# A convolution followed by an MLP: the transfers and the Pool casts of the opening in another order

## The chip, the core and the metric

The kernel runs on one core of a Trainium2 chip. The metric is the device time of one execution in microseconds (us); a kernel is given by the median of its runs.

## What is computed

The reference has two stages. The first is a causal convolution over 7 tokens whose weights depend only on the head (8 heads of 24 channels): a softmax over the 7 taps of each head, then a weighted sum of the last 7 tokens. The second is a two-layer MLP with the activation h cos h.

```python
w = softmax(weight)                                   # 8 heads x 7 taps
out[b, s, h, g] = sum_k w[h, k] * x_pad[b, s + k, h, g]   # x: 8 x 4096 x 192, 6 zero rows in front
x = out.reshape(32768, 192)
h = x @ w_in                                          # 192 -> 2048
return (h * cos(h)) @ w_out                           # 2048 -> 192, fp32
```

x holds 25 MB, w_in and w_out 1.57 MB each, all fp32; the matmuls run in bf16.

## The kernel before

**Units and tiles.** The 32768 tokens are cut into 32 units of 1024 tokens (x is loaded and convolved by units) and 64 tiles of 512 tokens (the MLP runs by tiles, two to a unit). The convolution of a unit is a set of matmuls against banded matrices (tile `band`, 128 x 8 x 256, built once from the softmaxed taps). Its result (`ct`) is transposed to channel-major form (`cT`), which feeds the first MLP matmul (`mm1`, eight pairs of h per tile, steps h0 to h7). ACT computes a cosine by its Sin function (`cs`, s0 to s7), DVE multiplies (`g`), and the second matmul (`mm2_step`, written m8, m12 and so on) accumulates into two PSUM banks, which ACT empties and SP stores.

**Order.** Every engine's order is the order in which the program records its instructions. Strings set it for a tile: `PE_ORDER` and `ACT_ORDER` from the third tile on, `PE_FIRST` and `ACT_FIRST` for the first two. In them h is an `mm1` step, c and d are halves of the next unit's convolution (ec, ed empty them on ACT), r is the second half of unit 0, m is `mm2`, s is a cosine. Three PSUM tiles (`h_pool`) hold h in turn, so an `mm1` step waits for the DVE product three steps back.

**Who casts.** Inputs arrive as fp32 and are cast to bf16 by other engines: x by Pool (`cast_unit`, L188; a piece of unit 0 by ACT), w_in in four pieces of two column groups each (pieces 0:2 on DVE at L286, 2:4 on Pool at L331, 4:6 and 6:8 on Pool at L442), w_out in two pieces on Pool (L447). Pool also doubles `ct` for the transposition (`double_unit`, L256) and mends `cT` (L268).

**Transfers.** SP and ACT issue transfers, each into a queue of its own, and both queues share 16 DMA engines. An instruction on SP that waits holds all that SP issues after it. In the opening SP issues, in this order: the first half of x's unit 0 (0.39 MB), piece 0:2 of w_in (0.39 MB, two transfers of 64 partitions each), the second half of unit 0, piece 2:4, piece 4:8 (0.79 MB), and w_out (1.57 MB in four). ACT issues the taps and then all of x's unit 1 (0.79 MB) with its edge rows (0.1 MB). Each transfer signals on one of eight completion semaphores in turn, so it also waits until the transfer eight before it has landed.

**The first 40 us.** Three plus eleven dummy matmuls (`keep_warm`) run while the taps are softmaxed. `mask`, a 0/1 pattern built by Pool on 32 partitions and copied by DVE to the other three quarters (L143), is multiplied with the taps (`prod`, L276) and reduced (`diag`, L279); 16 small casts (L284) put `diag` into `band`, dealt in turn to DVE, ACT and Pool. `conv_first` convolves the first half of unit 0, and `turn_first` transposes it by matmuls. The second half is convolved in tile 0 (`conv_rest`, step r) and transposed by a DMA (`turn_unit`, L262). Behind that transposition SP loads units 2 and 3. All casts that follow stand on Pool in one line, in this order: second half of unit 0; w_in 2:4; the doubling of unit 0; w_in 4:6 and 6:8; unit 1; w_out twice; the doubling of unit 1; units 2 and 3.

Of the kernel before, what the change touches and what calls it, by code (L numbers as in the profile page):

```python
# [9 lines left out]
BF16 = mybir.dt.bfloat16  # L10
AF = mybir.ActivationFunctionType
ALU = mybir.AluOpType
# [4 lines left out]
def kernel(  # L17
# [8 lines left out]
    nc = tc.nc  # L26
    B, S, D = x.shape
    H, K = weight.shape
# [5 lines left out]
    NB = T // 128  # L34
# [12 lines left out]
    consts = ctx.enter_context(tc.tile_pool(name="consts", bufs=1))  # L47
# [13 lines left out]
    HQ = H // 4  # L61
# [18 lines left out]
    w_src = moe_w_in.rearrange("(m k) (t f) -> t m k f", k=NC, t=2)  # L80
    HP = NP // 2

    def load_w(j0, j1):
        for t in range(2):
            nc.sync.dma_start(out=w_f[64 * t : 64 * t + 64, :, j0:j1, :].rearrange("p k j f -> p k (j f)"),
                              in_=w_src[t, :, :, j0 * 128 : j1 * 128])

    load_unit(0, 0, NB)
    load_w(0, 2)
    load_unit(0, NB, UB)  # L90
    load_w(2, 4)
    load_w(4, 8)
    wo_f = consts.tile([128, NP, 2, D], FP32)
    wo_src = moe_w_out.rearrange("(i j p) d -> p j i d", i=2, p=128)

    def load_wo(q):
        for i in range(2):
            nc.sync.dma_start(out=wo_f[:, q * HP : (q + 1) * HP, i], in_=wo_src[:, q * HP : (q + 1) * HP, i])

    load_wo(0)  # L100
    load_wo(1)


    one = consts.tile([128, 1], FP32)
# [5 lines left out]
    def keep_warm(n):  # L110
        for _ in range(n):
# [26 lines left out]
    nc.gpsimd.affine_select(out=mask[0:32], in_=mask[0:32], compare_op=ALU.not_equal, fill=1.0, base=1 - K,  # L138
                            pattern=[[1, K], [1, E]], channel_multiplier=-1)
# [44 lines left out]
    def cast_unit(u, n0=0, n1=UB + 1, copy=nc.gpsimd.tensor_copy):  # L184
        bf[u] = xb0 if u == 0 else xbf_pool.tile([128, UB + 1, D], BF16, name="x_bf")

        o = 1 if u == 0 else 0
        copy(out=bf[u][:, n0 + o : n1 + o, :].rearrange("p n (h k r) -> p (n h) k r", k=NC, r=R),  # L188
             in_=x_tiles[u][:, n0:n1, :].rearrange("p n (h r k) -> p (n h) k r", k=NC, r=R))
# [76 lines left out]
    def mend_edges(u):  # L266
# [9 lines left out]
    nc.vector.tensor_tensor(out=prod, in0=mask.rearrange("p k (o e) -> p o e k", o=1).to_broadcast([128, HQ, E, K]),  # L276
                            in1=wn.rearrange("p h (o k) -> p h o k", o=1).to_broadcast([128, HQ, E, K]), op=ALU.mult)
    diag = consts.tile([128, HQ, E], FP32)
    nc.vector.tensor_reduce(out=diag, in_=prod, axis=mybir.AxisListType.X, op=ALU.add)  # L279

    three = [nc.vector.tensor_copy, nc.scalar.copy, nc.gpsimd.tensor_copy]
    for i in range(16):
        q, rows = divmod(i, 4)
        three[i % 3](out=band[32 * rows : 32 * rows + 32, HQ * q : HQ * (q + 1), 32 * rows : 32 * rows + E],  # L284
                     in_=diag[32 * q : 32 * q + 32])
    nc.vector.tensor_copy(out=w[:, :, 0:2], in_=w_f[:, :, 0:2])  # L286
    cast_unit(0, NB, UB)
# [41 lines left out]
    turn_first(0)  # L329
    turn_first(1)  # L330
    nc.gpsimd.tensor_copy(out=w[:, :, 2:4], in_=w_f[:, :, 2:4])  # L331

# [57 lines left out]
    def store(t, b0=0, b1=2):  # L390
# [13 lines left out]
    ACT_FIRST = ["s0a s0b s1 s2 s3 s4 s5 ed1 ed2 s6 ec1 ec2 s7", "s0 s1 s2 s3 s4 ed1 ed2 s5 s6 ec1 ec2 P s7"]  # L404

    HALVES = {"": (0, NB), "a": (0, NB // 2), "b": (NB // 2, NB)}
    step = 0
    for t in range(NT + 2):
        u, second = divmod(t, TPU)
        cu, cc = (u + TPU, second) if t >= TPU else (1 + t, 1)  # L410
        conv = {"c": conv_part(cu, cc, ring_banks if t else o_banks, t < TPU) if cu < NU else iter(())}
        if t < TPU:
            conv["d"] = conv_part(cu, 0, ring_banks if t else o_banks, True)
        act, done, h = (ACT_ORDER if t > 1 else ACT_FIRST[t]).split(), set(), {}

        def flush():
            while act:
                k = act[0]
                need = {"P": "p", "Q": "q", "e": k[1:2] + "2"}.get(k[0], "h" + k[1:])
                if need not in done:  # L420
                    return
                act.pop(0)
                if k == "P" and 0 <= t - 1 < NT:
                    evac(t - 1, 0)
                elif k == "Q" and 0 <= t - 2 < NT:
                    evac(t - 2, 1)
                elif k[0] == "e":
                    next(conv[k[1]], None)
                elif k[0] == "s" and t < NT:
                    gcu(t, int(k[1]), h.pop(k[1:]), *HALVES[k[2:]])  # L430

        for k in (PE_ORDER if t > 1 else PE_FIRST[t]).split():
            if k[0] == "h" and t < NT:
                h[k[1:]] = mm1(t, int(k[1]), *HALVES[k[2:]])
            elif k[0] in conv:
                next(conv[k[0]], None)
            elif k == "r":
                conv_rest()
                double_unit(0, NB, UB)
                turn_unit(0, NB, UB)  # L440
                for j in (4, 6):
                    nc.gpsimd.tensor_copy(out=w[:, :, j : j + 2], in_=w_f[:, :, j : j + 2])  # L442
                cast_unit(1)
                load_unit(2)
                load_edges(2)
                for q in range(2):
                    nc.gpsimd.tensor_copy(out=wo[:, q * HP : (q + 1) * HP], in_=wo_f[:, q * HP : (q + 1) * HP])  # L447
            elif k[0] == "m":
                for q in range(step, step + int(k[1:])):
                    mm2_step(q)  # L450
                step += int(k[1:])
            elif k[0] == "p":
                assert step % (2 * STEPS) == 0
            elif k[0] == "q":
                assert step % (2 * STEPS) == STEPS
            done.add(k)
            flush()

            if k == "q":
                if second == 0 and t and u + 1 < NU:  # L460
                    turn_unit(u + 1)
                    mend_edges(u + 1)
                if t == 1:
                    turn_unit(1)
                    cast_unit(3)
                    mend_edges(1)
                if second == 0 and u + 3 < NU:
                    cast_unit(u + 3)
                if second == 1 and t > 1 and cu < NU:
                    double_unit(cu)  # L470
                if t == NT + 1:
                    store(NT - 1, 1, 2)
            if k == "p":
                if t < NT + 1 and 0 <= t - 2:
                    store(t - 2)
                if t == NT:
                    store(NT - 1, 0, 1)
                if second == 1 and u + 4 < NU:
                    load_unit(u + 4)
                    load_edges(u + 4)  # L480
        if t == 0:
            double_unit(1)
            load_unit(3)
            load_edges(3)
            cast_unit(2)
        if t == 1:
            double_unit(2)
# [30 lines left out]
```

## Time and profile before

| | |
|---|---|
| median of 8 runs | 725.96 us (725.02 to 726.35) |
| the profiled execution: own time, span | 725.02 us, 723.3 us |
| time outside the span | 1.7 us |
| PE busy | 709.3 us (98% of the span) |
| DVE, ACT, Pool busy | 613.7 us, 617.2 us, 150.2 us |
| PE busy from 40 to 715 us | 674.44 of 675 us |
| moved | 86.04 MB, 119 GB/s in the mean |

All positions in the text are microseconds from the start of the span. The span and what lies around it make the execution's own time; the profiled execution is one of the faster ones of its kernel (0.94 us under the median), so a change is worked out inside the span and then set against the median. "Idle before" in a row is the time for which the engine stood still ahead of that instruction, and the arrow names what ended it; where several things were waited for, it names the one that came last.

### The profile page before, as it was taken

What the parts mean: (1) busy time and instruction counts of PE and PEld (TensorE: products, weight loads), DVE (VectorE), ACT (ScalarE), POOL (GpSimd) and SP (SyncE); (2) the same over time, 40 slices, a digit from 0 to 9 for tenths busy, and PEclk for the clock granted to TensorE, in tenths of its full rate; (3) what the DMA queues carried; (4) which work ended last, traced back from release to release, by engine and by line L of the source; (5) the groups of instructions that cost most, each with busy time, mean ns of one, the idle gap of its engine ahead of it and who ended that gap; (6) DMA issues with size and microseconds to landing.
All of it is one profiled execution on the core that took longest, in us unless ns stands there. A gap on an engine that the chain in (4) does not pass through costs nothing.

```text
span 723.3 us, 26324 instructions
## 1 busy us (share of the span) xinstructions
PE 709.3 (98%) x11826; PEld 530.7 (73%) x11826; DVE 613.7 (85%) x538; ACT 617.2 (85%) x781; POOL 150.2 (21%) x125
## 2 busy tenths in 40 slices
PE   7799999999999999999999999999999999999997
PEld 3477777777777777777777777777777777777776
DVE  6778888888888888888888888888888888888983
ACT  5788888888888888888888888888888888888883
POOL 3731122210222211122210222220222211121000
PEclk9999999999999999999999999999999999999999
DMA  9945444555443555443555443565443555424312
GB/s 211 225 122 138 105 117 91 127 144 138 105 117 89 129 143 139 100 119 93 128 144 140 104 116 91 127 144 139 105 117 90 128 143 139 101 71 91 76 46 68
DMA packets 184497, 86.04 MB, mean 119 GB/s; under 512 B 111680, under 2 KB 184000, under 8 KB 184384
## 3 DMA queue, kind: packets, MB, share of 16 engines
q1 hardware_dynamic: 183200, 83.47, 47.5%
q8 instruction: 92, 1.51, 0.8%
q10 hardware_dynamic: 1184, 0.89, 0.5%
q14 instruction: 21, 0.17, 0.1%
HBM read 31.36 MB, written 25.17 MB: 78 GB/s over the span
## 4 chain that ended last, share of the span: by engine, by line
PE 95%; DMA 2%; POOL 1%; DVE 1%; ACT 0%; SPq 0%; issue 0%; DVEq 0%; POOLq 0%
PE o_ps L376 46%; PE h L346 45%; PE h L199 3%; DMA w_f<-in_moe_w_in_dram 1%; DMA x_f<-in_x_dram 1%; POOL x_bf L188 1%; PE h L376 0%; DVE g L357 0%; ACT cs L353 0%; POOL w L442 0%; DVEq L513 0%; SPq L262 0%; SPq L75 0%; ACT o_sb L388 0%; DVE ct L304 0%
## 5 line engine op out<-in xcount | busy, mean ns | idle before, releaser
L357 DVE TENSOR_TENSOR g<-h,cs 128x1024 bf16<-128x1024 f32 (+1 forms) x513 | 603.8, 1218 | 95.7 <-ACT cs L353 91.0
L353 ACT ACTIVATE cs<-h 128x1024 bf16<-128x1024 f32 (+1 forms) x513 | 511.6, 1026 | 61.4 <-PE h L346 54.2
L376 PE MATMUL o_ps<-wo,g 64*128 64x192 bf16 x8128 | 423.9, 243 | 1.5 <-ACT o_sb L388 0.6
L376 PEld LDWEIGHTS <-g 64*128 64x128 bf16 x8192 | 362.2, 94 | 85.6 <-SPq L173 1.2
L346 PE MATMUL h<-cT,w 64*128 64x512 bf16 (+1 forms) x3078 | 399.7, 377 | 2.2 <-POOL w L442 1.9
L346 PEld LDWEIGHTS <-w 64*128 64x128 bf16 x3078 | 154.8, 94 | 88.0 <-POOL w L442 2.4
L268 POOL COPY cT<-cT 128x144 bf16<-128x144 bf16 x31 | 9.5, 307 | 497.7 <-DMA cT<-ct 377.1
L188 POOL CAST x_bf<-x_f 128x1728 bf16<-128x1728 f32 (+2 forms) x33 | 81.3, 2463 | 4.4 <-DMA x_f<-in_x_dram 4.4
L214 ACT CAST ct<-h 128x432 bf16<-128x432 f32 x120 | 56.4, 522 | 27.0 <-PE h L199 26.9
L388 ACT COPY o_sb<-o_ps 128x384 f32<-128x384 f32 x127 | 60.1, 473 | 4.9 <-PE o_ps L376 4.9
L256 POOL COPY ct<-ct 128x1728 bf16<-128x1728 bf16 (+1 forms) x32 | 51.3, 1602 | 24.1 <-ACT ct L214 20.1
L199 PE MATMUL h<-x_bf,band 64*128 64x216 bf16 (+1 forms) x472 | 42.7, 254 | 0.5 <-POOL x_bf L188 0.5
L199 PEld LDWEIGHTS <-band 64*128 64x128 bf16 (+1 forms) x496 | 22.6, 96 | 6.4 <-issue 3.8
L112 PE MATMUL o_ps<-zero 128*128 128x512 bf16 x14 | 5.3, 547 | 1.3 <-DVE zero L107 1.3
L376 PE MATMUL h<-wo,g 64*128 64x192 bf16 x64 | 5.8, 243 | 0.0
L112 PEld LDWEIGHTS <-zero 128*128 128x128 bf16 x14 | 1.6, 127 | 3.7 <-issue 2.1
L199 PE MATMUL o_ps<-x_bf,band 128*128 128x96 bf16 (+1 forms) x24 | 2.5, 271 | 1.8 <-POOL x_bf L188 1.8
L214 ACT CAST ct<-o_ps 128x432 bf16<-128x432 f32 (+1 forms) x6 | 2.4, 457 | 1.1 <-PE o_ps L199 1.1
L447 POOL CAST wo<-wo_f 128x1536 bf16<-128x1536 f32 x2 | 2.9, 1472 | 0.0
L122 ACT ACT_TABLE_LOAD x1 | 1.3, 1283 | 1.4 <-PEq L502 1.4
L312 PE MATMUL h<-ident,ct 128*128 128x128 bf16 x9 | 0.8, 221 | 1.7 <-DVE ct L304 1.2
L388 ACT COPY o_sb<-h 128x384 f32<-128x384 f32 x1 | 0.5, 478 | 2.4 <-PE h L376 2.4
(47 smaller groups left out, 28.5 us busy)
## 6 DMA issues: line engine op xcount, KB each, us to landing
out_dram<-o_sb SPq DMA_DIRECT2D x63, 384.0 KB
x_f<-in_x_dram SPq DMA_DIRECT2D x30, 768.0 KB
x_f<-in_x_dram SPq DMA_DIRECT2D x30, 96.0 KB
wo_f<-in_moe_w_out_dram SPq DMA_DIRECT2D x4, 384.0 KB
x_f<-in_x_dram SPq DMA_DIRECT2D x2, 384.0 KB
w_f<-in_moe_w_in_dram SPq DMA_DIRECT2D x4, 192.0 KB
x_f<-in_x_dram ACTq DMA_DIRECT2D x1, 768.0 KB
w_f<-in_moe_w_in_dram SPq DMA_DIRECT2D x2, 384.0 KB
```

Of the source, the lines that this page charges most:

```text
L112: nc.tensor.matmul(out=idle, lhsT=zero[:, 0:128], rhs=zero, start=True, stop=True)
L188: copy(out=bf[u][:, n0 + o : n1 + o, :].rearrange("p n (h k r) -> p (n h) k r", k=NC, r=R), in_=x_tiles[u][:, n0:n1, :].rearrange("p n (h ...
L199: return nc.tensor.matmul(out=ps[i // 2][:, 0 : (n1 - n0) * 2 * G].rearrange("p (n k i r) -> p i n k r", n=n1 - n0, k=NC, i=2)[:, i % 2], ...
L214: copy(o[:, :, 0, :], i[:, :, 0, :])
L256: nc.gpsimd.tensor_copy(out=ct[:, n0:n1, :, 1, :], in_=ct[:, n0:n1, :, 0, :])
L268: nc.gpsimd.tensor_copy(out=cT[u][:, 0:UB, :, 0 : K - 1], in_=cT[u][:, UB].rearrange("p c (n t) -> p n c t", t=16)[:, :, :, 8 : 8 + K - 1])
L346: nc.tensor.matmul(out=h[:, i, n0 * 128 : n1 * 128], lhsT=w[rows, k, j, :], rhs=c[rows, m0 + n0 : m0 + n1, k, :], start=(k == 0), stop=(k ...
L353: nc.scalar.activation(out=cs[:, :, part], in_=h[:, :, part], func=AF.Sin, bias=math.pi / 2.0, scale=1.0)
L357: nc.vector.tensor_tensor(out=g_tiles[t][:, 2 * j : 2 * j + 2, part], in0=h[:, :, part], in1=cs[:, :, part], op=ALU.mult)
L376: m = nc.tensor.matmul(out=o_ps[tt, b][:, si * D : (si + 1) * D], lhsT=g_tiles[tt][rows, f, s * 128 : (s + 1) * 128], rhs=wo[rows, f // 2, ...
L388: nc.scalar.copy(o_sb[t][:, 2 * b : 2 * b + 2, :].rearrange("p s d -> p (s d)"), o_ps.pop((t, b))[:, 0 : 2 * D])
L447: nc.gpsimd.tensor_copy(out=wo[:, q * HP : (q + 1) * HP], in_=wo_f[:, q * HP : (q + 1) * HP])
```

## The change

It touches only the opening.

1. Piece 0:2 of w_in is issued by ACT, behind the taps and the first function-table load. Unit 1 and its edges, issued there before, come after the softmax's exponential on ACT's queue.
2. SP issues both halves of unit 0 at once, then piece 2:4. Piece 4:8 and w_out stand behind an SP instruction that waits for `diag`.
3. `mask` is stored with the tap as its innermost dimension, and its three copies are made by Pool, not DVE. `prod` reads it in storage order.
4. The first half of unit 0 is cast by ACT whole (768 elements a partition; before, 384 on ACT and 384 on Pool).
5. The 16 casts into `band` go 7 to DVE, 3 to ACT, 6 to Pool (before 6, 5, 5).
6. Pool's line of casts becomes: second half of unit 0; w_in 2:4; unit 1; w_in 4:6 and 6:8; the doubling of unit 0; w_out twice; and on as before.
7. In tile 0 the first half of unit 1's convolution (d1, d2) comes before h5 on PE, and its emptying after s4 on ACT.

```diff
-    def load_w(j0, j1):
+    def load_w(j0, j1, queue=nc.sync):
...
     load_unit(0, 0, NB)
-    load_w(0, 2)
     load_unit(0, NB, UB)
-    load_w(2, 4)
-    load_w(4, 8)
...
-    load_wo(0)
-    load_wo(1)
...
     nc.scalar.activation(out=scrap, in_=one, func=AF.Exp)
-    load_unit(1, queue=nc.scalar)
-    load_edges(1, queue=nc.scalar)
+    load_w(0, 2, nc.scalar)
...
-    mask = consts.tile([128, K, E], BF16)
+    mask = consts.tile([128, E, K], BF16)
     nc.gpsimd.memset(mask[0:32], 0.0)
...
+    for q in range(1, 4):
+        nc.gpsimd.tensor_copy(out=mask[32 * q : 32 * q + 32], in_=mask[0:32])
     band = consts.tile([128, H, 256], BF16)
     nc.vector.memset(band, 0.0)
-    for q in range(1, 4):
-        nc.vector.tensor_copy(out=mask[32 * q : 32 * q + 32], in_=mask[0:32])
...
     nc.scalar.activation(out=wexp, in_=wexp, func=AF.Exp)
     nc.scalar.activation(out=scrap, in_=one, func=AF.Sin)
+
+    load_unit(1, queue=nc.scalar)
+    load_edges(1, queue=nc.scalar)
+    load_w(2, 4)
...
-    cast_unit(0, 0, NB // 2, nc.scalar.copy)
-    cast_unit(0, NB // 2, NB)
+    cast_unit(0, 0, NB, nc.scalar.copy)
...
-    nc.vector.tensor_reduce(out=diag, in_=prod, axis=mybir.AxisListType.X, op=ALU.add)
-    three = [nc.vector.tensor_copy, nc.scalar.copy, nc.gpsimd.tensor_copy]
-    for i in range(16):
+    summed = nc.vector.tensor_reduce(out=diag, in_=prod, axis=mybir.AxisListType.X, op=ALU.add)
+    tc.add_manual_dep(nc.sync.nop().ins, summed.ins.name, sync_dep, reason="order of the transfers")
+    load_w(4, 8)
+    load_wo(0)
+    load_wo(1)
+    three = {"D": nc.vector.tensor_copy, "A": nc.scalar.copy, "P": nc.gpsimd.tensor_copy}
+    for i, k in enumerate("DPDPDPADPDPADPAD"):
...
     nc.gpsimd.tensor_copy(out=w[:, :, 2:4], in_=w_f[:, :, 2:4])
+    cast_unit(1)
+    for j in (4, 6):
+        nc.gpsimd.tensor_copy(out=w[:, :, j : j + 2], in_=w_f[:, :, j : j + 2])
...
-    PE_FIRST = ["h0a h0b h1 r h2 h3 h4 h5 d1 d2 h6 c1 c2 h7 p m12",
+    PE_FIRST = ["h0a h0b h1 r h2 h3 h4 d1 d2 h5 h6 c1 c2 h7 p m12",
...
-    ACT_FIRST = ["s0a s0b s1 s2 s3 s4 s5 ed1 ed2 s6 ec1 ec2 s7", ...
+    ACT_FIRST = ["s0a s0b s1 s2 s3 s4 ed1 ed2 s5 s6 ec1 ec2 s7", ...
...
                 turn_unit(0, NB, UB)
-                for j in (4, 6):
-                    nc.gpsimd.tensor_copy(out=w[:, :, j : j + 2], in_=w_f[:, :, j : j + 2])
-                cast_unit(1)
```

More of the change, by code (lines that the diff above doesn't have):

```diff
@@ L81 @@
     HP = NP // 2
-    def load_w(j0, j1):
+    def load_w(j0, j1, queue=nc.sync):
         for t in range(2):
-            nc.sync.dma_start(out=w_f[64 * t : 64 * t + 64, :, j0:j1, :].rearrange("p k j f -> p k (j f)"),
+            queue.dma_start(out=w_f[64 * t : 64 * t + 64, :, j0:j1, :].rearrange("p k j f -> p k (j f)"),
                               in_=w_src[t, :, :, j0 * 128 : j1 * 128])
     load_unit(0, 0, NB)
-    load_w(0, 2)
     load_unit(0, NB, UB)
-    load_w(2, 4)
-    load_w(4, 8)
     wo_f = consts.tile([128, NP, 2, D], FP32)
@@ L135 @@
     E = 32 + K - 1
-    mask = consts.tile([128, K, E], BF16)
+    mask = consts.tile([128, E, K], BF16)
     nc.gpsimd.memset(mask[0:32], 0.0)
     nc.gpsimd.affine_select(out=mask[0:32], in_=mask[0:32], compare_op=ALU.not_equal, fill=1.0, base=1 - K,
-                            pattern=[[1, K], [1, E]], channel_multiplier=-1)
+                            pattern=[[1, E], [1, K]], channel_multiplier=-1)
+    for q in range(1, 4):
+        nc.gpsimd.tensor_copy(out=mask[32 * q : 32 * q + 32], in_=mask[0:32])
     band = consts.tile([128, H, 256], BF16)
     nc.vector.memset(band, 0.0)
-    for q in range(1, 4):
-        nc.vector.tensor_copy(out=mask[32 * q : 32 * q + 32], in_=mask[0:32])
     nc.gpsimd.memset(xb0[:, 0, :], 0.0)
@@ L269, in mend_edges @@
                               in_=cT[u][:, UB].rearrange("p c (n t) -> p n c t", t=16)[:, :, :, 8 : 8 + K - 1])
-    cast_unit(0, 0, NB // 2, nc.scalar.copy)
-    cast_unit(0, NB // 2, NB)
+    cast_unit(0, 0, NB, nc.scalar.copy)
     prod = consts.tile([128, HQ, E, K], BF16)
-    nc.vector.tensor_tensor(out=prod, in0=mask.rearrange("p k (o e) -> p o e k", o=1).to_broadcast([128, HQ, E, K]),
+    nc.vector.tensor_tensor(out=prod, in0=mask.rearrange("p (o e) k -> p o e k", o=1).to_broadcast([128, HQ, E, K]),
                             in1=wn.rearrange("p h (o k) -> p h o k", o=1).to_broadcast([128, HQ, E, K]), op=ALU.mult)
     diag = consts.tile([128, HQ, E], FP32)
-    nc.vector.tensor_reduce(out=diag, in_=prod, axis=mybir.AxisListType.X, op=ALU.add)
-    three = [nc.vector.tensor_copy, nc.scalar.copy, nc.gpsimd.tensor_copy]
-    for i in range(16):
+    summed = nc.vector.tensor_reduce(out=diag, in_=prod, axis=mybir.AxisListType.X, op=ALU.add)
[5 more added lines that the diff above has]
+    for i, k in enumerate("DPDPDPADPDPADPAD"):
         q, rows = divmod(i, 4)
-        three[i % 3](out=band[32 * rows : 32 * rows + 32, HQ * q : HQ * (q + 1), 32 * rows : 32 * rows + E],
+        three[k](out=band[32 * rows : 32 * rows + 32, HQ * q : HQ * (q + 1), 32 * rows : 32 * rows + E],
                      in_=diag[32 * q : 32 * q + 32])
@@ L400 @@
     ACT_ORDER = "s0 ec1 ec2 s1 Q s2 s3 s4 s5 P s6 s7"
-    PE_FIRST = ["h0a h0b h1 r h2 h3 h4 h5 d1 d2 h6 c1 c2 h7 p m12",
+    PE_FIRST = ["h0a h0b h1 r h2 h3 h4 d1 d2 h5 h6 c1 c2 h7 p m12",
                 "h0 m8 h1 m12 q h2 h3 h4 m4 d1 d2 m8 h5 m8 h6 c1 c2 m8 h7 m4 p m8"]
-    ACT_FIRST = ["s0a s0b s1 s2 s3 s4 s5 ed1 ed2 s6 ec1 ec2 s7", "s0 s1 s2 s3 s4 ed1 ed2 s5 s6 ec1 ec2 P s7"]
+    ACT_FIRST = ["s0a s0b s1 s2 s3 s4 ed1 ed2 s5 s6 ec1 ec2 s7", "s0 s1 s2 s3 s4 ed1 ed2 s5 s6 ec1 ec2 P s7"]
     HALVES = {"": (0, NB), "a": (0, NB // 2), "b": (NB // 2, NB)}
```

## The prediction

> **What bounds the kernel now.** I read the busy shares and the table by stage first, then PE's waits, Pool's line in time, the chain of work, and the transfers.
>
> ```profile
> 40.00:715.00 675.00, 674.44 (x11459) 509.69 (x11457) 585.45 (x497) 588.93 (x737) 127.74 (x94) 1.00 0.47 115
> ```
>
> Second number: PE busy. From 40 us on PE is never without work, so a start that is earlier by d ends earlier by d. The question is what d is. PE's waits up to 42 us:
>
> ```profile
> PE h L346 <- POOL w L442: 1.9, 1, 1.9
> PE o_ps L199 <- POOL x_bf L188: 1.8, 1, 1.8
> ...
> PE h L312 <- DVE ct L304: 1.2, 1, 1.2
> ```
>
> The two longest are for casts on Pool. Pool in time (start, length, what, idle before):
>
> ```profile
> 11.80 1.21 POOL L188 CAST x_bf<-x_f 128x768 bf16<-128x768 f32 x1 [3.10 <-DMA x_f<-in_x_dram]
> 13.48 0.83 POOL L331 CAST w<-w_f 128x768 bf16<-128x768 f32 x1 [0.47 <-DMA w_f<-in_moe_w_in_dram]
> 18.01 0.83 POOL L256 COPY ct<-ct 128x768 bf16<-128x768 bf16 x1 [3.70 <-DVE ct L214]
> 18.78 1.60 POOL L442 CAST w<-w_f 128x768 bf16<-128x768 f32 x2
> 20.32 2.51 POOL L188 CAST x_bf<-x_f 128x1728 bf16<-128x1728 f32 x1
> 22.77 2.88 POOL L447 CAST wo<-wo_f 128x1536 bf16<-128x1536 f32 x2
> ```
>
> Pool stands idle for 3.70 us ahead of the doubling at 18.01, with three casts behind it that PE needs. The chain of work, and the transfers up to 9.7 and from 5 to 8 us:
>
> ```profile
> 18.78 1.61 POOL w L442 x2
> 20.39 1.13 SPq L262
> ...
> 22.18 5.21 DMA x_f<-in_x_dram
> ```
>
> ```profile
> DMA packets 2440, 1.91 MB, mean 197 GB/s; under 512 B 80, under 2 KB 2440, under 8 KB 2440
> ...
> q10 hardware_dynamic: 1184, 0.89, 35.9%
> ```
>
> ```profile
> q10 hardware_dynamic: 582, 0.44, 62.1%
> q1 hardware_dynamic: 323, 0.31, 42.8%
> ```
>
> q10 is ACT's queue: unit 1 (0.89 MB with edges) is all in by 9.7 us and lies unused until 20.32. It delays piece 0:2 of w_in, for which DVE waits until 10.04.
>
> **The change part by part.** The goal is the first PE step that nothing earlier can delay: h0 of tile 1, now at 26.46 (its transposed input comes from the DMA transposition).
>
> *Softmax to band.* Taking three mask copies (0.99) off DVE frees wmax from 3.53 to about 3.35, since its matmul ends at 3.29: at most 0.2. The product wn took 0.60 where its like took 0.17, beside Pool's cast at 4.47 to 5.16; that cast goes to ACT: 0.43. prod took 1.17 for 532 elements, and the reduction over the same 532 takes 0.71; in storage order I take 0.71, with 1.17 as the other end: 0.46 or 0. So `diag` comes 1.1 us earlier (0.6 to 1.1). Pool's three mask copies lie between its rows of 0.31 (144 elements) and 0.83 (768): some 0.4 each, done by 4.4, ahead of prod at 4.7. DVE's seven casts instead of six cost 0.27. `band` is complete at about 7.95 instead of 8.76. ACT's whole cast of 768 elements costs between 0.80 (its 768-element copy from PSUM) and 1.40 (twice its 0.70); I take 1.2, so 5.58 to 6.8; dummy matmuls hold PE until 7.1 anyway. The three band casts behind it on ACT (0.27 each) end by 7.7. Gain for `conv_first`: about 0.8.
>
> *Piece 0:2 on ACT's queue.* ACT issues it at 1.5, where unit 1 stood. Ahead of it or beside it are now x's first and second halves and some of piece 2:4, 1.26 MB with itself. The run moved 0.82 MB by 5 us and 248 GB/s from there: 6.8, with a lag of the last DMA engine 7.5 to 8.5. So DVE no longer waits until 10.04; its cast (0.69) and the copy of `ct` behind it come about 1.1 earlier, and h0a moves from 12.21 to about 11.1. The Trainium skill, "DMA: Bandwidth & Descriptors", section "Issuing engines are not separate DMA queues", says that starting transfers from several engines saves only their issue time, as all run on the same DMA engines. By that rule the swap itself is worth at most the 1.31 us that SP's two issues took, and what counts is which bytes stand in front, as I have counted.
>
> *Unit 1 later on ACT's queue.* It is issued behind the exponential (now 3.95), that is at about 3.9. The price is here. In front of it or beside it now go both halves of x's unit 0, pieces 0:2 and 2:4 (4 x 0.393 MB), itself (0.885), and a share of piece 4:8. Where x and w_in competed (5 to 8 us) they moved 0.44 and 0.31 MB, so unit 1 gets about 150 of 250 GB/s: of its last 0.42 MB's time piece 4:8 takes 0.28 MB. Together 2.74 MB. The run had 1.91 MB at 9.7 and then 225 GB/s: 9.7 + 0.83 / 0.225 = 13.4. If piece 4:8 gets nothing it is 12.2, if all of it goes first 16.0. With 0.5 for the slowest DMA engine I take 13.9.
>
> *Piece 4:8 held until `diag` (6.1).* Queued behind that wait on SP: w_out's four transfers, the transposition, units 2 and 3. It costs nothing as long as SP's queue still has piece 2:4 to move, until about 10.6. In bytes nothing is ahead of piece 4:8 that was not ahead before: 3.24 MB, at 13.4 2.74 MB of them and then 196 GB/s: 16.0, with the lag 16.4.
>
> *Pool's new order.* Six band casts and the second half of unit 0 (1.21) are done before 9.7, piece 2:4 by about 12. Unit 1: 14.0 to 16.5. Pieces 4:6 and 6:8 (1.60): 16.5 to 18.1. The doubling (0.83, its input is ready by then): to 19.0, where it now ends at 18.84. w_out: to 21.9 instead of 25.65. So both waits of PE go: h4 can start at 17.4 (now 19.66), and d1 finds unit 1 cast (it came at 22.89).
>
> *What is late next.* ACT runs s4, ed, s5, s6, ec1 from 18.1: 1.02 + 0.94 + 2.0 + 0.47 gives 22.5. Then m12 can start at 22.6 (now 25.70), takes 1.0, and h0 of tile 1 could start at 23.6. But its input is the transposition: issued at 19.05 instead of 18.86, 2.65 long, 21.7. Its data ended 2.1 after its issue in this run; the next transposition, at 29.98 for 4.11, released Pool at 37.69, 1.0 behind its last data. Nobody waited for the first one, so 2.1 to 3.1: 23.8 to 24.8, middle 24.3. Gain 26.46 - 24.3 = 2.2. The loads behind the transposition move by +0.2: unit 2 is cast at 30.5 instead of 30.3, and its reader d1, at 32.84, may come 2.2 earlier (30.64). It just fits, so this chain allows no more than 2.3 either.
>
> The sum: the profiled execution would be 725.02 - 2.2 = 722.8; set against the median, 725.96 - 2.2 = 723.8.
>
> **The rivals.** *Unit 1 lands late.* Every us after 13.9 delays Pool's whole line, the doubling and the transposition by one. At 16.0 the gain is 0.1; at 14.65 it is 1.45, which is 0.2%, about what a measurement of this kernel can tell from no change. Against it: ACT's queue got more than SP's from 5 to 8 us. Time about 725.1.
>
> *A cold PE.* Granted clock (after POOL's column) in two stretches:
>
> ```profile
> 9.40:12.80 3.40, 1.65 (x25) 0.94 (x21) 2.52 (x4) 1.60 (x4) 1.00 (x1) 1.00 1.13 239
> 12.80:16.20 3.40, 3.29 (x28) 2.00 (x28) 1.53 (x4) 2.17 (x3) 1.03 (x2) 0.50 1.09 207
> ```
>
> After 3.4 us at 49% busy PE had half the clock for 3.4 us. Now it was followed by waits, so it cost little; behind 24 us it would cost half of 3.4: 2.2 - 1.7 = 0.5, 725.5. PE will be sparse between 15.5 and 24. The Trainium skill, "TensorE: Matmul & The Clock Gate", Part 1, gives an idle window of about 3.4 us as what lowers the clock; by that rule no such stretch arises and the cost is nothing. The row shows the drop without an idle stretch.
>
> *Pool blocked by the held transfer (slower).* Piece 4:8 now stands in Pool's line before the doubling, which did not need it. If SP's queue runs dry behind the `diag` wait, or w_in moves slower, h0 of tile 1 starts 7.9 after it lands (1.6 + 0.85 + 2.65 + 2.1 to 3.1). It decides from 18.6, where that makes 26.5. The worst place is beside the end of w_out, 20.7: 28.6, so 2.1 slower, 728.1. Against it: 16.4 by bytes.
>
> *More than forecast.* Piece 4:8 and unit 1 land a little earlier and the transposition's signal comes at 2.1: 3.2 at most, as w_out's bytes still stand in front of it: 722.8.
>
> **How the numbers follow.** Forecast 0.56; more 0.08; unit 1 late 0.13; cold PE 0.11; blocked Pool 0.12. Faster by over 0.2%: 0.64. Within: 0.24. Slower: 0.12. The range, 722.7 to 725.9, holds the forecast with its ends and the two rivals near no change, and leaves out the slow one.
>
> **What would show it.** Right: Pool casts unit 1 at 14 ± 1, the doubling ends at 19, no PE wait on L442's work above 0.3, h0 of tile 1 at about 24.3 with an idle ahead of it that a DMA ended. Wrong: the cast of unit 1 after 16, a half clock after 20 us, or PE waiting again before 40 us for a cast of unit 2 or 3 by more than 0.5.

## The result, and the profile after

The changed kernel takes 722.53 us in the median of 11 runs (722.01 to 727.35); the kernel before took 725.83 us in 31 runs on the same chip. The ratio is 0.9963, with a 95% interval of 0.9952 to 0.9975, so the change gains 1.8 to 3.5 us: faster, as forecast. The profiled execution of the changed kernel took 722.64 us (forecast for it: 722.8) with a span of 720.9 us (723.3 before). Set against the median, the forecast was 723.8 us and the range began at 722.7: the median lies 1.3 us below the one and 0.2 below the other, while the forecast gain of 2.2 us lies within the interval. Where the rest may come from is told further down.

First the stretch in which PE should never be without work:

```profile
40.00:715.00 675.00, 674.42 (x11454) 509.67 (x11449) 583.95 (x496) 588.36 (x737) 127.63 (x94) 1.00 0.47 114
```

It is as before. The cosines on ACT and the products on DVE, matched one by one in the two traces, run 1.96 us earlier from 33 us to 710 us, to two decimals. So, between these two executions, the whole gain of the kernel's work is made before 33 us and handed through. The span is 2.4 us shorter; the other 0.44 us is the end, from the start of the last copy to the store's completion (3.6 us after, 4.1 before), and is no work of this change.

Pool in time (start, length, what, and the idle before with what ended it):

```profile
9.31 0.83 POOL L333 CAST w<-w_f 128x768 bf16<-128x768 f32 x1 [0.29 <-DMA w_f<-in_moe_w_in_dram]
14.20 2.53 POOL L186 CAST x_bf<-x_f 128x1728 bf16<-128x1728 f32 x1 [4.06 <-DMA x_f<-in_x_dram]
17.36 1.60 POOL L336 CAST w<-w_f 128x768 bf16<-128x768 f32 x2 [0.62 <-DMA w_f<-in_moe_w_in_dram]
18.90 0.83 POOL L254 COPY ct<-ct 128x768 bf16<-128x768 bf16 x1
20.59 1.47 POOL L449 CAST wo<-wo_f 128x1536 bf16<-128x1536 f32 x1 [0.86 <-DMA wo_f<-in_moe_w_out_dram]
```

In these rows Pool stands idle only for transfers. Unit 1, which was cast at 20.32, is cast at 14.20, and behind it w_in's piece 4:6 and w_out are cast as they land. PE's waits up to 42 us (total, times, longest):

```profile
PE h L351 <- POOL w L336: 1.6, 1, 1.6
...
PE o_ps L381 <- ACT ct L212: 1.0, 1, 1.0
PE h L197 <- POOL x_bf L186: 1.0, 1, 1.0
```

Three waits remain that belong to this change: h4 for piece 4:6 of w_in (until 18.24), m12 for ACT's emptying of `ct` (until 23.27), and d1 of tile 1 for the cast of unit 2 (until 30.89). What they hang on is told by the chain of work (start, length, what):

```profile
6.57 10.67 DMA w_f<-in_moe_w_in_dram
...
18.13 0.83 POOL w L336
18.95 0.78 POOL ct L254
19.75 2.28 SPq L260
...
22.71 5.45 DMA x_f<-in_x_dram
...
28.32 2.54 POOL x_bf L186
30.89 0.53 PE h L197 x4
```

From issue of piece 4:8 to d1 of tile 1 the chain has one thread: the piece lands, Pool casts and doubles, SP issues the transposition and then unit 2 behind it, unit 2 lands, Pool casts it. At h0 of tile 1 the changed kernel was 2.40 us ahead (24.06 against 26.46); at d1 it is 1.95 us ahead (30.89 against 32.84), and that is what stays. In what follows the mark is the first copy of a result by ACT, behind all waits of the opening: 38.39 before, 36.43 after.

### The profile page after: what moved, and what is told of

The parts are those of the page before. It is cut to its first block, busy times and chain, and to the rows that moved or that the text cites. A ratio compares the mean times of both kernels' runs of the same rounds, so it can differ in the third digit from the quotient of the medians.

```text
span 720.9 us, 26325 instructions
## 1 busy us (share of the span) xinstructions
PE 708.9 (98%) x11826; PEld 530.7 (74%) x11826; DVE 611.9 (85%) x536; ACT 617.0 (86%) x779; POOL 151.8 (21%) x128
## 4 chain that ended last, share of the span: by engine, by line
PE 95%; DMA 2%; POOL 1%; DVE 1%; SPq 0%; ACT 0%; issue 0%; DVEq 0%; POOLq 0%
PE o_ps L381 46%; PE h L351 45%; PE h L197 3%; DMA w_f<-in_moe_w_in_dram 1%; DMA x_f<-in_x_dram 1%; PE h L381 0%; POOL x_bf L186 0%; SPq L260 0%; PE o_ps L107 0%; DVE g L362 0%; DVEq L515 0%; ACT cs L358 0%; ACT o_sb L393 0%; POOL w L336 0%; POOL ct L254 0%
## 5 line engine op out<-in xcount | busy, mean ns | idle before, releaser
L186 POOL CAST x_bf<-x_f 128x1728 bf16<-128x1728 f32 (+1 forms) x32 | 80.5, 2515 | 6.9 <-DMA x_f<-in_x_dram 6.8
```

## The experiments

Twelve kernels ran. A ratio is always against the kernel before on the same chip; the kernel before took 725.93, 725.67 and 726.12 us in the medians of the three groups.

### The parts alone

The change has three parts: **transfers** (what is issued where, with the wait on SP), **band** (mask, product, casts of the first half and of `band`), and **Pool's line** (unit 1 and pieces 4:6, 6:8 ahead of the doubling, with d1 d2 before h5 in tile 0). Four kernels each lack one part or two.

Run A: transfers and band, Pool's line as before.

```diff
-    cast_unit(1)
-    for j in (4, 6):
-        nc.gpsimd.tensor_copy(out=w[:, :, j : j + 2], in_=w_f[:, :, j : j + 2])
...
-    PE_FIRST = ["h0a h0b h1 r h2 h3 h4 d1 d2 h5 h6 c1 c2 h7 p m12",
+    PE_FIRST = ["h0a h0b h1 r h2 h3 h4 h5 d1 d2 h6 c1 c2 h7 p m12",
...
                 turn_unit(0, NB, UB)
+                for j in (4, 6):
+                    nc.gpsimd.tensor_copy(out=w[:, :, j : j + 2], in_=w_f[:, :, j : j + 2])
+                cast_unit(1)
```

> The changed kernel with its new transfers and its quicker band, but Pool's line and the steps of tile 0 in the old order (unit 0's doubling, w_in 4:6 and 6:8, then unit 1). Mark: the first copy out of an output bank on ACT (o_sb), at 38.39 us in the kernel before and 36.43 in the changed one; from there on both run in step. Theory 'Pool's order': unit 1 is cast only at about 19.0 to 21.5, d1 follows at 21.6 and m12 at 24.5, so the mark is at about 37.2 and some 0.8 us of the gain of 1.96 are lost. Theory 'transfers and band': the mark stays within 0.3 of 36.43.

Run B: Pool's line alone, transfers and band as before (the same lines of the diff, the other way round).

> The kernel before with Pool's new line and the new order of d1 and d2 alone; transfers, mask, cast and band as before. Theory 'Pool's order': h0a stays at 12.2, but unit 1 is cast at about 14.3 to 16.9, h4 starts at about 17.8 and m12 at 23.7; the transposition is issued at about 19.4. Mark at 36.4 to 36.7, nearly the whole gain. Theory 'transfers and band': mark at 37.6 or later, less than 0.8 gained.

Run C: transfers and Pool's line, band as before.

> The changed kernel with mask, the cast of unit 0's first half and the dealing of the band casts as before; transfers and Pool's order stay new. Theory 'Pool's order': diag and conv_first come about 1 us later, but PE waits 1.65 us for w_in 4:6 ahead of h4 in the changed kernel and takes it back there: mark 36.4 to 36.6. Theory 'transfers and band': the mark comes later by what diag loses, 37.2 to 37.5.

Run D: band and Pool's line, transfers as before.

> The changed kernel with the transfers of before (piece 0:2 of w_in and unit 1 where they stood, nothing held); quicker band and Pool's new order stay. Theory 'Pool's order': piece 0:2 lands at about 10 again and h0a is at about 12; unit 1 and piece 4:8 are there for Pool by 14.3 and 17: mark 36.3 to 36.7. Theory 'transfers': the order of landing is what the new line of Pool needs, mark at 37.2 or later.

| kernel | has | median, us | ratio (95%) | h0a | h4 | h0, tile 1 | d1, tile 1 | mark |
|---|---|---|---|---|---|---|---|---|
| before | | 725.93 | 1 | 12.21 | 19.66 | 26.46 | 32.84 | 38.39 |
| A | transfers, band | 723.83 | 0.9977 (0.9967 to 0.9987) | 11.43 | 18.88 | 25.67 | 32.04 | 37.60 |
| B | Pool's line | 723.03 | 0.9967 (0.9955 to 0.9978) | 12.18 | 17.76 | 24.02 | 30.74 | 36.28 |
| C | transfers, Pool's line | 722.52 | 0.9961 (0.9947 to 0.9975) | 11.84 | 18.32 | 24.11 | 30.59 | 36.12 |
| D | band, Pool's line | 723.66 | 0.9972 (0.9962 to 0.9981) | 13.41 | 19.13 | 25.36 | 31.73 | 37.28 |
| after | all | 722.53 | 0.9963 (0.9952 to 0.9975) | 11.01 | 18.24 | 24.06 | 30.89 | 36.43 |

Run B is the finding: three moved lines and two changed order strings give 2.9 of the 3.3 to 3.4 us. Run A, without them, gives 2.1, so the parts do not add up, and the intervals of A and B overlap; it is the marks that part them (2.1 us earlier in B, 0.8 in A). Of the marks expected, those of B and C were 0.1 and 0.3 too late, that of A 0.4 too early. Pool's line of run B:

```profile
14.17 2.55 POOL L188 CAST x_bf<-x_f 128x1728 bf16<-128x1728 f32 x1
16.88 1.60 POOL L334 CAST w<-w_f 128x768 bf16<-128x768 f32 x2 [0.16 <-DMA w_f<-in_moe_w_in_dram]
18.42 0.83 POOL L256 COPY ct<-ct 128x768 bf16<-128x768 bf16 x1
```

With the old transfers unit 1 is already in by 9.7 us, and Pool casts it from 14.17, just as late as in the changed kernel (14.20), because piece 2:4 of w_in comes later. Piece 4:6 is cast even sooner, at 16.88 instead of 17.36. The h0a that is 1.2 us earlier in the changed kernel is not passed on: PE ran at half the clock from 12.0 to 15.4 there, and at h4 both wait for piece 4:6 (1.65 and 1.55 us).

Run C says the same of the band: without it the mark is at 36.12 and the time the same. Run A gained 2.1 us in the median, more than its mark (0.8) shows; why is not shown. Its profile has the old wait in its old place, 2.2 us for piece 4:6, which was cast behind the doubling, ahead of which Pool had stood idle for 6.5 us.

Run D, with its mark at 37.28, went against the theory of Pool's order (36.3 to 36.7) and just met the rival (37.2 or later). In its profile the early band met late transfers: ACT and Pool were free early, but w_in's piece 0:2 and the second half of unit 0 came late (Pool cast the latter at 13.21 against 11.77 in run B with the same transfers), DVE waited for piece 0:2 ahead of its copy of `ct`, and PE waited 2.5 us for that. Why these transfers came later than in run B is not shown, and the clock weighs in it too: in the three stretches of 3.4 us from 9.4 us on, run D was granted 0.75, 0.50 and 0.74 of it, run B 1.00. B and D differ only in the band, and their intervals overlap, so that the band costs something there is not shown. Nor is what the transfers add to run B: 722.52 against 723.03 with intervals that overlap.

### d1 and d2 later: is unit 2 the last limit?

Run E: the first half of unit 2's convolution in tile 1 stands behind h5, so that PE asks for the cast of unit 2 later. Run F: the same, and d1 d2 before h4 in tile 0.

```diff
-                "h0 m8 h1 m12 q h2 h3 h4 m4 d1 d2 m8 h5 m8 h6 c1 c2 m8 h7 m4 p m8"]
+                "h0 m8 h1 m12 q h2 h3 h4 m4 m8 h5 d1 d2 m8 h6 c1 c2 m8 h7 m4 p m8"]
```

> The changed kernel with one more edit: in tile 1 the first half of unit 2's convolution (d1, d2) stands after h5, not before it, and its emptying on ACT after s5; eight mm2 steps that stood behind it come first. Nothing moves in the transfers or on Pool. Mark: first copy out of an output bank (38.39 before, 36.43 in the changed kernel). Theory 'unit 2's landing caps': d1 waits in the changed kernel until unit 2 is cast (30.86); 1 us later on PE it finds it ready, the wait goes, the mark is at about 36.0 and the time 0.45 lower. Theory 'PE's own work caps': mark stays at 36.4.

> As the run before, and in tile 0 d1 and d2 stand before h4, their emptying before s4, so that they fill the 1.65 us in which PE waits for w_in 4:6 and the 1.2 us in which ACT does. m12 should start at about 22.3 instead of 23.27. Theory 'transfers cap': h0 of tile 1 then waits for the transposition, which lands at about 24.0 (2.3 after its issue ends); mark no earlier than 35.8. Theory 'ACT's chain in tile 0 caps': h0 of tile 1 at about 23.1 and the mark at about 35.1.

Run E took 722.44 us (0.9953, 0.9936 to 0.9970), run F 722.47 us (0.9954, 0.9937 to 0.9971), on 6 runs each. The medians do not tell them from the changed kernel. Their profiled executions took 724.37 and 724.30 us, 1.8 to 1.9 us over their medians, and their marks are at 38.11 and 38.06, so for the limit they say nothing. They say something else. Run E's opening is the changed kernel's, instruction by instruction, and yet PE waited 3.85 us ahead of h4 instead of 1.65: h4 came 0.85 later, since piece 4:6 was cast at 18.20 instead of 17.36, and PE was done 1.35 sooner. Its windows (the number after the counts of the five engines is the granted clock, then DMA share and GB/s):

```profile
14.80:18.20 3.40, 0.44 (x6) 0.00 (x0) 3.37 (x5) 1.77 (x2) 2.51 (x1) 1.00 1.12 240
18.20:21.60 3.40, 2.51 (x12) 0.85 (x14) 0.00 (x0) 1.01 (x2) 3.40 (x4) 0.50 0.76 230
21.60:25.00 3.40, 3.40 (x18) 1.16 (x16) 2.34 (x2) 2.77 (x5) 1.86 (x2) 0.50 0.85 160
```

PE had been at full clock from 11 to 15 us, and after the wait it had half the clock for 6.8 us, in which all from h4 to just ahead of m12 lies. In the changed kernel's own profile the half clock fell from 12.0 to 15.4, ahead of the wait, where it cost nothing. This is the cold PE of the prediction, in an execution in which it counts.

### Six matmuls of zeros in the wait ahead of h4

```diff
-    PE_FIRST = ["h0a h0b h1 r h2 h3 h4 d1 d2 h5 h6 c1 c2 h7 p m12",
+    PE_FIRST = ["h0a h0b h1 r h2 h3 w h4 d1 d2 h5 h6 c1 c2 h7 p m12",
...
+            elif k == "w":
+                idle2 = o_pools[0].tile([128, T], FP32, name="o_ps0")
+                for _ in range(6):
+                    nc.tensor.matmul(out=idle2, lhsT=zero[:, 0:128], rhs=zero, start=True, stop=True)
```

> The changed kernel with six more matmuls of zeros (128x512, into the bank of the first idle matmuls) between h3 and h4 of tile 0, where PE waits 1.65 us for the cast of w_in's piece 4:6. They compute nothing that is used. At full clock six take 1.3 us and at half clock 2.6. Theory (PE waits there for data, not for its clock): first store copy 36.2 to 36.7, time as the changed kernel (722.2 to 722.9), h4 within 0.3 us of 18.24. What they could bring is that no half-clock stretch begins in that wait (16.6 to 18.2): in two profiled executions with an edit elsewhere it began there and lasted to 25 us, and the first store copy came at 38.1. Rival (they stand in h4's way, since PE takes them in order): h4 at 18.7 or later, first store copy 36.8 to 37.4, time 723.0 to 723.6.

It took 722.91 us (0.9961, 0.9949 to 0.9974): no difference to the changed kernel, as the theory had it (its mark, 35.88, was 0.3 earlier than it said). The profiled execution opened like run E's (the eleven idle matmuls of the opening took 4.64 us here, 4.85 in run E, 3.46 in the changed kernel; h0a 11.23 and 11.21), and so the two can be set side by side:

```profile
14.80:18.20 3.40, 1.92 (x13) 0.55 (x10) 3.40 (x5) 1.80 (x2) 3.39 (x3) 1.00 1.12 238
18.20:21.60 3.40, 3.38 (x30) 1.50 (x32) 1.23 (x1) 2.57 (x4) 2.87 (x3) 1.00 0.98 265
```

With the zeros PE was busy for 1.92 instead of 0.44 us of the same stretch, the clock stayed at 1.00, and the mark came at 35.88, where run E's came at 38.11. Not all of these 2.23 us is the clock: at h4 the two were already 0.93 apart (18.16 and 19.09), as piece 4:6 was cast 0.92 apart. From h4 to h0 of tile 1 it took 5.80 us here, 5.82 in the changed kernel and 7.27 in run E, so the half clock cost some 1.5 us. One execution of each is no proof, and the median did not move, so executions like run E's cannot be most of the changed kernel's. Here unit 2 was issued at 21.36 (the transposition's issue took 1.58 us, 2.28 in the changed kernel's profile) and cast by 30.22; d1 did not wait.

### Without the wait on SP, and with half of it

Run G takes the wait for `diag` away; the order of the issues in the program stays.

```diff
-    tc.add_manual_dep(nc.sync.nop().ins, summed.ins.name, sync_dep, reason="order of the transfers")
```

> The changed kernel without the SP instruction that holds piece 4:8 of w_in and w_out until diag. All theories that count bytes: the same bytes stand in front of everything, so no change: unit 1 cast at 13.2 to 14.3, mark 36.2 to 36.6. Theory 'the hold protects unit 1': without it piece 4:8 competes with unit 1 earlier, its cast comes at 15 or later and the mark at 37 or later.

727.79 us, 1.0023 (1.0013 to 1.0033): slower than the kernel before, with the mark at 41.59. The theory that counts bytes alone fell; the other, that the wait protects unit 1, held by its signs (a cast at 15 or later, a mark at 37 or later). ACT and Pool in its profile, one after the other:

```profile
10.03 1.22 ACT L186 CAST x_bf<-x_f 128x768 bf16<-128x768 f32 x1 [4.56 <-DMA w_f<-in_moe_w_in_dram]
```

```profile
19.74 2.51 POOL L186 CAST x_bf<-x_f 128x1728 bf16<-128x1728 f32 x1 [9.27 <-DMA x_f<-in_x_dram]
```

Two things went wrong at once. The transfers on SP now came early enough to take completion semaphores out of turn, so that unit 1's issue on ACT (5.96, in the changed kernel 3.75) had to wait for a half of unit 0 and its edges (9.29) for w_in's piece 0:2. ACT's cast of unit 0 stands behind them and came at 10.03 instead of 5.38. And the bytes of piece 4:8 were moved ahead of unit 1's and those of w_out beside them, so that Pool could cast unit 1 only at 19.74. To tell the two apart, run H lets SP go on at 4.56 (the product `wn`) instead of 5.90, when unit 1 has been issued.

```diff
-    nc.vector.tensor_tensor(out=wn, in0=wexp, ...
+    early = nc.vector.tensor_tensor(out=wn, in0=wexp, ...
...
-    tc.add_manual_dep(nc.sync.nop().ins, summed.ins.name, sync_dep, reason="order of the transfers")
+    tc.add_manual_dep(nc.sync.nop().ins, early.ins.name, sync_dep, reason="order of the transfers")
```

> The changed kernel, but SP's wait ahead of w_in's piece 4:8 is for wn (written at 4.39 to 4.56) and no longer for diag (5.90), so the piece is issued about 1.3 us earlier, while unit 1 is still issued before it on ACT's queue (3.75). The semaphores of the transfers are dealt in nearly the same order as with the full wait; the one difference is that the edges' issue on ACT waits for the second half of unit 0 instead of the first. Theory (the run without the wait lost 5 us because the early transfers on SP took the completion semaphores that unit 1 needs, so that unit 1 was issued late): unit 1 is issued in time here, Pool casts it at 14.2 to 15.0, unit 0's first cast on ACT comes at most 0.8 us later (up to 6.2), first store copy 36.4 to 37.3, time 722.5 to 723.4. Rival (it is the bytes: whatever of w_in is asked for before about 6 us is carried ahead of unit 1): unit 1 is cast at 17 or later, first store copy past 39, time 725.5 or more.

725.81 us, 1.0000 (0.9991 to 1.0008): the whole gain is gone, for 1.4 us of earlier issue. Unit 1 was issued at 3.76, in time, and yet:

```profile
16.99 2.50 POOL L186 CAST x_bf<-x_f 128x1728 bf16<-128x1728 f32 x1 [6.17 <-DMA x_f<-in_x_dram]
```

The theory (semaphores alone) falls, and the rival holds, just: 16.99 where it said 17 or later, mark 39.58 where it said past 39. The DMA queues from 11 to 16 us, run H first and the changed kernel second (q10 is ACT's):

```profile
q1 hardware_dynamic: 659, 0.88, 85.8%
q10 hardware_dynamic: 308, 0.22, 25.6%
```

```profile
q1 hardware_dynamic: 613, 0.90, 104.2%
q10 hardware_dynamic: 60, 0.04, 5.6%
```

From 11 us on the changed kernel has 0.04 MB of unit 1 and its edges left to move, run H 0.22 MB. At 12 us 0.87 of 0.88 MB were in there and 0.73 here, and of piece 4:8 already 0.22 and 0.33 MB. What of unit 1 was not through when the large packets of piece 4:8 came up got a fifth of the bytes in run H and took some 6 us. The one profile alone would not settle it: unit 1 was cast at 14.34 to 15.96 in runs E, J, K and the one with the zeros, which issue as the changed kernel does, but in run F's execution, which does too, at 17.39. In run C, whose late `diag` holds piece 4:8 until 7.06, it was cast earliest, at 13.24. That the wait matters is shown by the medians: with the full wait 722.4 to 722.9 (C, E, F, zeros, the changed kernel), without its last 1.4 us 725.81. The price in time has a second part: PE stood for 4.7 us ahead of h4, and then had half the clock from 19.6 to 26.4. How much each part costs was not separated. The clock is not all of it: four executions of run H with a mean clock of 0.997 took 724.25 to 725.48 us, seven of the changed kernel with 0.996 or 0.997 took 722.22 to 723.69. Nor was it separated whether the edges (issued 1.6 us later here, since they wait for the second half of unit 0) weigh in it.

### Both queues for each transfer

Run I splits w_in's halves, unit 0 and unit 1 between SP and ACT.

```diff
-    def load_w(j0, j1, queue=nc.sync):
-        for t in range(2):
-            queue.dma_start(...
+    def load_w(j0, j1, halves=(0, 1)):
+        for t in halves:
+            (nc.sync, nc.scalar)[t].dma_start(...
...
+    load_unit(1, 0, NB)
+    load_unit(1, NB, UB, queue=nc.scalar)
+    load_edges(1)
```

> The changed kernel with every load of the opening but w_out and the edges cut in two that run side by side: the halves of w_in by partitions (0 to 63 by SP, 64 to 127 by ACT), and units 0 and 1 by blocks. In the changed kernel a w_in transfer covers 64 partitions at a time and moves 217 to 225 KB per us when alone, against 320 to 330 for x and w_out on 128. Theory 'half the partitions set the rate': pieces 0:2, 2:4 and 4:8 move at about 300 or more, piece 4:8 lands some 1.5 to 2 us earlier than 17.3, and with it w_out, the transposition and unit 2; mark at 35.5 or earlier. Theory 'the rows of w_in set the rate': no change in the rate; mark at 36.4, or later, since ACT's issues delay the cast of unit 0.

724.08 us (0.9981, 0.9968 to 0.9994), 1.5 us above the changed kernel's median. ACT's cast of unit 0 stood behind an issue that waited until 7.17, PE waited 2.4 us for it, and piece 2:4 was cast at 12.05 instead of 9.31. The order of the bytes was not better, and nothing showed that w_in moves faster from two queues.

### Unit 2 earlier

Run J issues unit 2 on ACT's queue behind s4 of tile 0; run K also has d1 d2 later in tile 1, as run E.

```diff
             done.add(k)
             flush()
+            if t == 0 and k == "h4":
+                load_unit(2, queue=nc.scalar)
+                load_edges(2, queue=nc.scalar)
...
-                load_unit(2)
-                load_edges(2)
```

> The changed kernel, but unit 2 and its edges are issued on ACT's queue behind gate 4 of tile 0 (about 19.3 to 20.6) instead of on SP's behind the transposition of unit 0 (22.14 and 22.71). Theory (unit 2's landing is the last wait of the opening; the DMA engines carry only the transposition's small packets from 21 to 23.6 and can take unit 2's bytes there): unit 2 lands 1 to 1.8 us earlier, its cast on Pool begins at 26.5 to 27.3 instead of 28.3, PE waits for it no more at d1 of tile 1 (1.0 now), first store copy 35.4 to 36.0, time 721.5 to 722.1. Rival (bytes are what bounds: unit 2 takes them from w_out's tail and from the transposition): w_out's second cast ends after 24.8 or the transposition lands after 24.6, unit 0's second tile starts at 24.6 to 25.6, and the first store copy stays at 36.2 to 37.2, time 722.3 to 723.3.

> The run before (unit 2 on ACT's queue), and conv d1 d2 of tile 1 also moved behind h5 there, so that PE needs unit 2's cast about 1.7 us later. If unit 2 is what ends last, the two remedies do the same and do not add: first store copy within 0.3 us of the run with unit 2 early, time 721.4 to 722.2. If unit 2 stays late in that run (its rival), the later place takes the wait away all the same, and the first store copy is 0.5 to 1.0 us earlier than there. If it is the transposition or w_out that has become late, the later place brings nothing, and the time stays at 722.3 to 723.3.

J took 727.84 us (1.0016, 1.0003 to 1.0029) and K 727.19 us (1.0011, 0.9999 to 1.0023). The remedy did what it said: unit 2 was cast from 25.61 and done at 28.11, 2.7 us earlier. But the transposition, issued at the same time as in the changed kernel, ended 6.41 us after its issue (chain of work, run J):

```profile
19.85 6.41 DMA cT<-ct
...
26.30 1.46 PE h L351 x5
```

In these 6.41 us all 0.88 MB of unit 2 and its edges were moved; that they went ahead of the transposition's own bytes is the likely reading. So far the rival held, with h0 of tile 1 at 26.30 where it said 24.6 to 25.6. What none had seen is the price, the mark at 41.93. PE waited twice in short order (1.16 us ahead of m12, 1.53 us for the transposition), and then had half the clock for some 10 us:

```profile
23.00:26.40 3.40, 1.26 (x14) 1.03 (x16) 2.84 (x3) 1.91 (x4) 3.10 (x3) 0.91 1.21 277
26.40:30.00 3.60, 3.60 (x20) 1.96 (x21) 1.13 (x1) 1.02 (x1) 2.13 (x2) 0.50 0.59 176
30.00:34.00 4.00, 4.00 (x24) 2.81 (x24) 1.32 (x2) 1.46 (x2) 2.10 (x1) 0.50 0.09 18
```

K's mark is at 42.05, within 0.3 of J's, but not for the reason given: unit 2 was early in both, and both paid for the transposition and the clock (h0 of tile 1 at 27.72, half clock from about 28.7 to 35.5). Nor is there a gain where the clock hardly fell: two of J's twelve executions had a mean clock of 0.999 and 0.998 and took 723.99 and 724.44 us, and the kernel with the zeros took 722.91 on the same chip.

No kernel here beats the changed one beyond the intervals.

## Why the prediction was right

**A start earlier by d ends earlier by d.** Held: 1.96 us from 33 to 710 us.

**Softmax to band, piece 0:2.** Sizes held: `diag` 1.24 earlier (1.1 forecast; `prod` took 0.48, not 0.71), ACT's whole cast 1.22 (1.2), conv_first at 6.83 (7.1), h0a at 11.01 (11.1). Piece 0:2 landed later than the 7.5 to 8.5 forecast: DVE waited 1.13 us for it and cast it at 8.93. The sum used none of this, and rightly: runs B and C show no gain from it.

**Unit 1 on ACT's queue.** Forecast to land at 13.9, cast at 14.20, and between 14.34 and 17.39 in the five other profiles with the same issues in front of it, so the bounds (12.2 to 16.0) were 1.4 short above. 0.87 of its 0.88 MB were in by 12; the last few packets kept Pool until 14.20. The forecast had the bytes come evenly to 13.4, with 0.5 for the slowest DMA engine: that the time came out right is luck, the working was right only in part.

**The wait on SP "costs nothing".** It costs nothing, but this is the step that the prediction read wrongly: it saw no use in the wait, and counted the bytes ahead of unit 1 without it. It had SP's queue busy with piece 2:4 until about 10.6; from 8 to 10 us SP's queue moved 0.02 MB and ACT's 0.54 MB, so unit 1 went through a gap that the wait had left. Run H shows that 1.4 us less of it cost all of the gain, and in the profiles of G and H unit 1 was cast at 19.74 and 16.99. That it lands at 14 because of the wait is what these bytes say, on few profiles: in run F's it was late with the wait too. The prediction had worked out what it would mean, "if all of it goes first 16.0", but tied it to ACT's queue and not to the wait.

**Piece 4:8.** Mis-sized by 1.0: cast at 17.36, not 16.4. From there all is late by 0.7 to 0.9: casts done at 18.96 (18.1), doubling at 19.73 (19.0), h4 at 18.24 (17.4), with 1.65 us of waiting where no more than 0.3 was to be seen, and m12 at 23.27 (22.6). The sign "no wait above 0.3" failed for this. The casts of w_out ended at 24.29, not 21.9, as Pool waited 0.86 and 0.76 us for its transfers; PE did not wait for them.

**The transposition.** Issued at 19.75 instead of 19.05, but 2.28 us long instead of 2.65, and its data was there by 24.06, when h0 of tile 1 began without a wait for it (forecast 24.3, with a wait that a DMA ended). m12, late by 0.7, was what h0 followed. So the gain at this place was 2.40 against 2.2 forecast: a late piece and a faster transposition cancelled, which is luck.

**Unit 2.** "It just fits, this chain allows no more than 2.3." The chain ended it, at 1.95: unit 2's cast was done at 30.86, not 30.5, and PE waited 1.0 us at d1 (0.5 before). By the sign given (more than 0.5) this would have spoken against the forecast. The mechanism was named, only its bound was 0.35 too wide.

**From the profile to the median.** The prediction took the gain of the profiled execution for that of the median. The profiled executions differ by 2.4 us, the medians by 3.3. It also wrote of the half clock that the kernel before had from 12.8 to 16.2 us that it cost little, as waits followed. This reading was wrong. In that execution's chain of work (start, length, what) the stretch lies on the way to the doubling, and so to the casts of piece 4:6 and of unit 1 behind it:

```profile
12.91 2.12 PE h L346 x12
15.05 1.03 ACT cs L353
16.11 1.23 DVE g L357
17.33 0.54 DVE ct L214 x2
```

In run B, whose clock stayed at 1.00, the same twelve matmuls took 1.15 us, so up to 1 us of the 2.1 between its mark and the old one may be the clock and not the order. But with Pool's new line these casts no longer stand behind that chain: run C and the changed kernel had the half clock from 12.0 to 15.4 and their marks at 36.12 and 36.43, run B had none and its mark at 36.28. The executions beside the experiments point the same way. Of the kernel before, six with a mean clock of 0.998 or more took 723.95 to 725.08 us, and 46 with 0.996 or 0.997 took 725.7 in the median; of the changed kernel, three took 722.01 to 723.15 and seven 722.22 to 723.69. So part of the gain seems to be that a half clock in the opening no longer delays Pool, which the sum did not have. It was not tested, say by holding the clock up in the kernel before.

**The cold PE.** Given 0.11 and 1.7 us. Behind 16 us no half clock fell in the profiled execution of the changed kernel, but it did in those of six others (runs E to H behind a single wait of PE of 3.2 to 4.7 us, J and K behind two shorter ones in short order). Run E against the zeros makes it some 1.5 us, near the 1.7. The Trainium skill, "TensorE: Matmul & The Clock Gate", Part 1, says that the clock falls after an idle window of about 3.4 us, and that the windows run freely, wherever the kernel starts. The length of the half-clock stretches agrees (3.4 us and about two or three times that), and so does the opening that differs from one execution to the next. That the window must be idle is not borne out: the clock fell after 1.65 us of work in 3.4 (before) and in a stretch with 1.26 (run J). Nor does the busy time alone decide: it stayed up after 1.92 (the zeros), but also after 1.57 (before, 16.2 to 19.6 us).

**The blocked Pool.** The terms of its 7.9 add up to 7.2 to 8.2, 7.7 in the middle; nothing hangs on the 0.2.

**Bytes, not queues.** The rule of the Trainium skill, "DMA: Bandwidth & Descriptors", section "Issuing engines are not separate DMA queues", weighed in the prediction, held where it could be seen: in run G from 13 to 17 us the two queues moved 0.66 and 0.65 MB, beside each other. The gain of the transfers over run B, 0.5 us with overlapping intervals, is within the 1.31 us that the rule allowed.

## What to carry to other kernels

Where one engine does all casts in a line, order the line by when its inputs land: here that alone gives 2.9 of 3.3 us, and what the finer work on the transfers and on the band adds to it is within the uncertainty, though without the new order it gives 2.1. When an opening is bound by bytes, a transfer that is held back is a tool: giving up 1.4 us of holding cost all of the gain, and the bytes say that the next unit went through a gap in the other queue. And a wait of PE of some 3 us can be paid twice, as in runs E to H, where the matmuls behind it ran at half the clock for 3.4 us or more: a transfer moved forward to save 1 us (run J) put the mark back by 5.5.

## What the runs showed of the hardware that was not expected

- Two queues did not always share the DMA engines evenly: from 11 to 16 us in run H q10 (packets of 768 bytes) moved 0.22 MB beside 0.88 MB of q1, most of it in packets of 2048 bytes. With packets of 768 bytes on both (run G, 13 to 17 us) it was 0.66 beside 0.65 MB. That the size of the packets is the reason was not tested.
- 99% of unit 1 was in by 12.0, but Pool could cast it only from 14.2; in the six profiles with the same issues it was between 14.2 and 17.4.
- An issue can hold up its engine's other work: ACT stood 4.56 us in run G for a transfer of w_in that its next cast, of x, does not read.
- The half clock lasted 3.4 us, 6.8 us or, in run J, some 10 us, and began in different places in executions with the same opening.
